# Attention pieces woven into an MLP: one piece per slot, and product drains issued ahead of the woven pieces

## The chip, the cores and the metric

The kernel runs on one core of a Trainium2 chip. The metric is device time in microseconds (us) of one execution. Most tables quote the median of all executions of a kernel.

For differences below 1% I rely on *batch lengths*: the time from the first up-projection matmul of a batch (tile `ph`) to that of the next, read from the timeline. Of the kernel before there is one, and at 594.98 us it was faster than every one of its timed executions (595.57 to 601.82 us).

## The reference, cut to what matters

```python
q_n, k_n = rmsnorm(q, g_q), rmsnorm(k, g_k)         # q, k, v: 8 batches, 12 heads, 448 tokens, 64 dims
attn = softmax(scale * q_n @ k_n.T)                 # per head
x = (attn @ v)  -> (8, 448, 768)
h = x.transpose(0, 2, 1) @ U @ V                    # low-rank mixing over tokens, rank 32
u = x + h.transpose(0, 2, 1)
out = u + np.maximum(u @ w_ch1, 0) @ w_ch2          # 768 -> 3072 -> 768
```

## The kernel before

TensorE (PE) is the scarce engine. The MLP of batch b is written as a Python generator that yields after every six matmuls; `weave` runs it and, between yields, issues pieces of the attention of batch b+1, in proportion to their weights. A *slot* is the place between two weighted pieces. `FA` is the share of the MLP's work over which attention is spread; the low-rank mixing of batch b+1 follows over a share of 0.09. Each engine has a queue of its own, filled in the order in which the code issues instructions; the timelines below show VectorE (DVE) working in that order.

The down-projection of an odd batch, and two of the three token tiles of an even one, uses seven products instead of eight per pair of token tiles, with sums of weights (`weight_sums`, once, in batch 1) and of activations (`act_sums`) on DVE. Each product has a *drain*, the instructions that take its PSUM tile away.

```python
def product(ps, lhs, rhs, first, last, again=False):
    for c in range(NC):                              # 12 matmuls
        nc.tensor.matmul(ps, lhs[:, c, :], rhs[:, c, :], ...)
        if c % 6 == 5:
            yield HALF                               # also after the last one: pieces come before the drain

def pair(b, i, then=None):
    ...
    yield from product(pa, A12, B21, False, True, True)
    nc.vector.tensor_tensor(A12, A12, A11, OP.subtract)
    o11 = out_tile(); nc.vector.tensor_add(o11, pa, X[0][0]); store(b, i, 0, o11)
    yield from product(pb, A21, B12, False, True, True)
    o22 = out_tile(); nc.vector.tensor_add(o22, pb, se)
    nc.gpsimd.tensor_tensor(o22, o22, X[1][1], OP.add); store(b, i + 1, 1, o22)
    if then:
        then()                                       # act_sums for the second pair of tiles
    yield from product(pe, A12, B22, False, True, True)
    ...

def attention(b, extra={}):                          # p: pair of heads, t = p // 2: their loaded tile
    for p in range(b * 6, b * 6 + 6):
        add(2 if p == 6 else 1, scores, p, (0, 1)); add(0, expo, p, 0); add(.5, expo, p, 1)
        add(.5, transposes, p + 1)                   # from p + 1 = 14 on: a transposing DMA on the sync queue
        ...                                              # cut here and below: mix_u, loads, casts
        if t + 1 < NT and not odd: add(0, reduce, t + 1, ALL, (1,))      # row sum of squares of K
        if p % 6: add(2, values, p - 1, 0)
        add(0, gains, p + 1)                         # qkT *= gg on DVE: waits for that DMA
        if t + 1 < NT and odd: add(0, scale, t + 1, 1) ...
        add(1, scores, p, (2, 3)); add(0, expo, p, 2); add(.5, expo, p, 3)
        if t + 1 < NT and not odd: add(0, rsqrt, t + 1)
        if p % 6: add(1.5, values, p - 1, 1)
        if t + 1 < NT and not odd:
            add(0, scale, t + 1, 0) ...; add(0, squares, t + 2, ALL, (0,))
        if p in (12, 13, 14):                        # four weight sums at a time, eight at p = 14
            for i in range(4): add(0, weight_sums, ...)
        if t + 2 < NT and odd:
            add(0, reduce, t + 2, ALL, (0,)); add(0, squares, t + 2, ALL, (1,))
```

## Time and profile before

| | before |
|---|---|
| time, median | 597.1 us |
| span of the profiled execution | 593.2 us |
| PE / DVE / ScalarE (ACT) busy | 96% / 66% / 47% |
| head (up to the first `ph`) | 45.84 us |
| batches 0 to 7 | 66.89, 79.27, 62.94, 74.74, 62.95, 74.74, 63.42, 62.39 us |

Even batches have 384 tokens to work on and odd ones 512, so the lengths alternate; batch 1 also carries the weight sums, and batch 7 has no attention to weave.

From the page of the kernel before: its span, the first line of part 1 (busy us, share, instructions) and of part 4 (the chain of work that ended last, by engine).

```profile
span 593.2 us, 11361 instructions
...
PE 568.0 (96%) x4613; PEld 312.9 (53%) x4613; DVE 393.1 (66%) x811; ACT 278.6 (47%) x413; POOL 85.9 (14%) x122
...
PE 74%; DVE 14%; ACT 4%; DMA 3%; issue 2%; POOL 1%; DVEq 0%; ACTq 0%; POOLq 0%; SPq 0%
```

PE looks full. It is not: a quarter of the chain runs elsewhere. The list of waits of PE says what it waited for (us in total, times, longest one); note that it leaves out the pieces of a wait that the modelled end of the matmul before covers, so the true holes are some 0.15 us longer each.

```profile
PE ph L468 <- DVE hT L473: 3.4, 5, 1.2
PE sc L273 <- ACT E L278: 2.4, 6, 0.6
PE ph L468 <- DMA u<-x: 1.8, 3, 1.1
PE o L299 <- DVE xs L306: 1.7, 1, 1.7
...
PE pb L404 <- DVE o L434: 1.3, 3, 0.4
```

The fourth line and the longest wait of the first, 1.2 us in batch 1, come from the weight sums; the rest of the first line is 0.5 to 0.8 us each in batch 0 and the even batches. The timeline of DVE in batch 1 (start, us, line, operation, count) shows a burst of four sums, then a row sum, and the ReLU `hT` that PE waits for only behind both. PE stood still for 1.3 us up to 134.9 us.

```profile
130.38 2.75 DVE L394 TENSOR_TENSOR Tw<-w2b,Tw 128x1152 bf16<-128x1152 bf16 x4
133.05 1.21 DVE L231 TENSOR_REDUCE rstd<-sq 112x16 f32<-112x1024 f32 x1
134.18 0.68 DVE L473 TENSOR_SCALAR hT<-ph 128x512 bf16<-128x512 f32 x1
```

The line for `pb` is one wait in each odd batch. Timeline of DVE, and below it the matmuls that wait: the product `pb` was done before 308.7 us (`pe`, the next one, starts at 308.65), but its drain (`o<-pb,se`) runs at 310.60, behind three instructions of a values piece and a row sum.

```profile
308.85 0.18 DVE L302 RECIPROCAL rec<-o 128x4 f32<-128x4 f32 x1 [0.59 <-PE o L299]
309.06 0.36 DVE L303 TENSOR_TENSOR x<-o,rec 128x192 bf16<-128x192 f32 x1
309.34 0.21 DVE L306 TENSOR_TENSOR xs<-o,rec 64x64 bf16<-64x64 f32 x1
309.47 1.20 DVE L231 TENSOR_REDUCE rstd<-sq 112x16 f32<-112x1024 f32 x1
310.60 0.54 DVE L434 TENSOR_TENSOR o<-pb,se 128x384 f32<-128x384 f32 x1
...
311.19 1.14 PE L404 MATMUL pb<-Tw,hT 128*128 128x384 bf16 x6 [0.43 <-DVE o L434]
```

### The profile page before, as it was taken

How to read it: one execution, taken by the hardware profiler on the slowest of the kernel's cores; microseconds unless marked ns; L12 is line 12 of the kernel's file. 1: busy time of each engine (PE TensorE's matmuls, PEld its weight loads, DVE VectorE, ACT ScalarE, POOL GpSimd, SP SyncE). 2: the span in 40 equal slices, each digit the busy share in tenths (PEclk: the TensorE clock that was granted, in tenths of full speed). 3: DMA queues.
4: the chain of work that ended last, by engine and by line, in shares of the span. 5: the costliest groups of instructions: out<-in, count | busy, mean ns of one | idle time of the engine just before them, and what ended most of it. 6: DMA issues, size and time to landing. Idle time of an engine off the chain costs nothing.

```text
span 593.2 us, 11361 instructions
## 1 busy us (share of the span) xinstructions
PE 568.0 (96%) x4613; PEld 312.9 (53%) x4613; DVE 393.1 (66%) x811; ACT 278.6 (47%) x413; POOL 85.9 (14%) x122
## 2 busy tenths in 40 slices
PE   6899999998899999999999999999999999999997
PEld 2465555544465555644456555644455555654464
DVE  6968886388875678737767487757667577453452
ACT  5846662257531676256541576336662366302200
POOL 5652420023020000000010000100002000000010
PEclk9999999999999999999999999999999999999999
DMA  9999989342454345644526345555335432040021
GB/s 212 236 240 236 216 152 189 92 109 32 109 142 100 82 95 133 147 99 109 125 77 127 85 113 123 136 122 125 80 61 157 100 94 33 28 108 0 1 51 56
DMA packets 103648, 67.22 MB, mean 113 GB/s; under 512 B 54716, under 2 KB 102060, under 8 KB 103596
## 3 DMA queue, kind: packets, MB, share of 16 engines
q1 hardware_dynamic: 93988, 56.77, 41.4%
q0 software_dynamic: 9376, 9.44, 9.7%
q8 instruction: 36, 0.59, 0.4%
q10 hardware_dynamic: 232, 0.30, 0.2%
q14 instruction: 16, 0.13, 0.1%
HBM read 52.19 MB, written 11.01 MB: 107 GB/s over the span
## 4 chain that ended last, share of the span: by engine, by line
PE 74%; DVE 14%; ACT 4%; DMA 3%; issue 2%; POOL 1%; DVEq 0%; ACTq 0%; POOLq 0%; SPq 0%
PE ph L468 27%; PE pb L404 10%; PE pa L404 7%; PE o L299 7%; PE po L404 7%; PE pe L404 6%; PE sc L273 5%; DVE rstd L231 3%; DVE qkn L244 3%; ACT E L278 2%; PE pu L337 2%; DMA u<-x 2%; DVE Tw L394 1%; DVE x L303 1%; DVE hT L473 1%
## 5 line engine op out<-in xcount | busy, mean ns | idle before, releaser
L468 PE MATMUL ph<-u,w1b 128*128 128x512 bf16 (+1 forms) x1128 | 232.9, 353 | 5.4 <-DVE hT L473 3.4
L278 ACT ACTIVATE E<-sc 112x896 bf16<-112x896 f32 x184 | 159.5, 915 | 45.1 <-PE sc L273 44.4
L468 PEld LDWEIGHTS <-w1b 128*128 128x128 bf16 x1128 | 103.2, 98 | 111.5 <-issue 25.6
L404 PEld LDWEIGHTS <-hT 128*128 128x128 bf16 x1080 | 101.2, 98 | 72.9 <-issue 9.7
L471 ACT ACTIVATE hT<-ph 128x384 bf16<-128x384 f32 (+1 forms) x95 | 51.5, 544 | 140.4 <-PE ph L468 135.8
L473 DVE TENSOR_SCALAR hT<-ph 128x512 bf16<-128x512 f32 (+1 forms) x93 | 57.9, 623 | 50.5 <-PE ph L468 49.9
L299 PEld LDWEIGHTS <-E 112*128 112x128 bf16 x1472 | 58.3, 98 | 17.4 <-DVE xs L306 3.5
L223 ACT ACTIVATE sq<-qk 112x1024 f32<-112x1024 f32 x36 | 37.8, 1049 | 58.2 <-DVE rstd L231 40.2
L273 PE MATMUL sc<-qkT 64*112 64x448 bf16 x384 | 60.8, 374 | 3.7 <-ACT E L278 2.4
L681 POOL COPY scratch<-qkn 1x1 bf16<-1x1 bf16 x44 | 18.3, 416 | 314.9 <-DVE qkn L244 313.4
L244 DVE TENSOR_TENSOR qkn<-qk,rstd 112x512 bf16<-112x512 f32 x84 | 56.3, 709 | 10.4 <-issue 6.0
L299 PE MATMUL o<-va,E 112*128 112x65 bf16 x1440 | 61.0, 194 | 1.7 <-DVE xs L306 1.7
L404 PE MATMUL po<-w2b,hT 128*128 128x384 bf16 x288 | 52.2, 326 | 0.6 <-DVE hT L473 0.6
L231 DVE TENSOR_REDUCE rstd<-sq 112x16 f32<-112x1024 f32 x40 | 48.5, 1212 | 4.9 <-ACT sq L223 3.7
L404 PE MATMUL pa<-w2b,hT 128*128 128x384 bf16 x264 | 49.5, 326 | 0.0
L404 PE MATMUL pb<-Tw,hT 128*128 128x384 bf16 x264 | 48.0, 326 | 1.3 <-DVE o L434 1.3
L302 DVE RECIPROCAL rec<-o 128x4 f32<-128x4 f32 x96 | 17.1, 178 | 35.6 <-PE o L299 35.4
L273 PEld LDWEIGHTS <-qkT 64*112 64x112 bf16 x384 | 19.6, 124 | 36.8 <-issue 31.9
L303 DVE TENSOR_TENSOR x<-o,rec 128x192 bf16<-128x192 f32 x96 | 34.3, 358 | 3.7
L435 POOL TENSOR_TENSOR o<-o,x 128x384 f32<-128x384 f32 x11 | 12.6, 1146 | 160.6 <-DVE o L434 160.6
L339 DVE TENSOR_TENSOR x<-pu,x 128x768 bf16<-128x768 f32 (+1 forms) x27 | 23.3, 866 | 8.2 <-PE pu L337 7.9
L404 PE MATMUL pe<-Tw,S 128*128 128x384 bf16 x132 | 24.3, 326 | 0.0
(106 smaller groups left out, 426.0 us busy)
## 6 DMA issues: line engine op xcount, KB each, us to landing
qk<-in_q_dram SPq DMA_DIRECT2D x21, 448.0 KB, 6.0
vt<-in_v_dram SPq DMA_DIRECT2D x20, 448.0 KB, 5.0
qk<-in_k_dram SPq DMA_DIRECT2D x19, 448.0 KB, 3.9
w2b<-in_moe_w_ch_dram POOLq DMA_DIRECT2D x6, 768.0 KB, 9.7
w1b<-in_moe_w_ch_dram POOLq DMA_DIRECT2D x2, 1536.0 KB, 22.3
out_dram<-o SPq DMA_DIRECT2D x15, 168.0 KB, 2.6
out_dram<-o SPq DMA_DIRECT2D x16, 144.0 KB, 2.1
out_dram<-o SPq DMA_DIRECT2D x15, 120.0 KB, 2.0
```

Source lines behind the costliest of these rows:

```text
L223: nc.scalar.activation(sqs[t, s][:, hs], qks[t, s][:, hs], AF.Square)
L231: nc.vector.tensor_reduce(rstds[t][:, s, hs].rearrange("p h j -> p (h j)"), sqs[t, s][:, hs].rearrange("p h (j d) -> p (h j) d", d=D), AX, ...
L244: nc.vector.tensor_tensor(qkn[:, s].rearrange("p j h d -> p h j d"), qks[t, s][:, hp].rearrange("p h (j d) -> p h j d", d=D), rstd[:, s, h ...
L273: nc.tensor.matmul(sc[:, hh, 0:S], kT[pp, kc * SP:(kc + 1) * SP], qT[pp, :], start=True, stop=True)
L278: nc.scalar.activation(E_of(p)[:, :, PAD + kc * S:PAD + (kc + 1) * S], scs.pop((p, kc))[:, :, 0:S], AF.Exp, scale=float(D) ** 0.5)
L299: nc.tensor.matmul(o[:, i, :], E[:, hh, c:c + P], va[:, hl, kc, :], start=(kc == 0), stop=(kc == NJ - 1))
L303: nc.vector.tensor_tensor(x3[:, :, d0:d0 + D], o[:, t0:t0 + 3, 0:D], rec[:, t0:t0 + 3].rearrange("p c -> p c ()").to_broadcast([P, 3, D]), ...
L339: nc.vector.tensor_add(xv, pu[rows, 0:n, 0:HALF], xv)
L404: nc.tensor.matmul(ps, lhs[:, c, :], rhs[:, c, :], start=first and c == 0, stop=last and c == NC - 1, skip_group_check=again)
L468: nc.tensor.matmul(ph, w1b[:, dc, hc * P:(hc + 1) * P], u[:, dc, :], start=(dc == 0), stop=(dc == KD - 1))
L471: nc.scalar.activation(hT[:, hc, 0:n], ph, AF.Relu)
L473: nc.vector.tensor_relu(hT[:, hc, 0:n], ph)
```

## The change

Its intent is to break up bunches. Seven things move (the share, the drains, the weight sums, squares, row sums, gains and transposes); no arithmetic is added or removed.

```diff
-    FA, FM, NPE, FA0 = 0.77, 0.09, 14, 0.66
+    FA, FM, NPE, FA0 = (0.74, 0.77), 0.09, 14, 0.66          # even, odd batches
 def product(...):
-            if c % 6 == 5:
+            if c == 5:                                         # the yield at the end moves to the callers,
                 yield HALF                                     # behind each drain:
 def pair(b, i, then=None):
         nc.gpsimd.tensor_tensor(o22, o22, X[1][1], OP.add)
         store(b, i + 1, 1, o22)
         if then:
             then()
+        yield HALF
         yield from product(pe, A12, B22, False, True, True)
  ...    (the same after every other drain, in pair, single and batch 0)
 def attention(b, extra={}):
+        def sums(p, n):                                        # one weight sum at each of four places
+            f = {12: 0, 13: 1, 14: 3, 15: 2}.get(p)
+            if f is not None:
+                add(0, weight_sums, f, 3 * n)
  ...
-            if p + 1 < NP:
+            if p + 1 < NP and (p + 1 >= NPE or not odd):
                 add(.5, transposes, p + 1)
-            if t + 1 < NT and not odd:
-                add(0, reduce, t + 1, ALL, (1,))
+            sums(p, 0)
+            if not odd and more:
+                add(0, squares, t + 1, ALL, (1,))              # squares of K, one slot later than before
+            if odd and more2:
+                add(0, squares, t + 2, ALL, (0,))
             if p % 6:
                 add(2, values, p - 1, 0)
-            if p + 1 < NP:
-                add(0, gains, p + 1)
+            sums(p, 1)
+            if not odd and more:
+                add(0, reduce, t + 1, ALL, (1,))
  ...        (scores, p, (2, 3) and their exponentials)
+            if p + 1 < NPE and odd:
+                add(.5, transposes, p + 1)
+            if p + 1 < NP:
+                add(0, gains, p + 1)                           # gains half a piece later
+            sums(p, 2)
             if p % 6:
                 add(1.5, values, p - 1, 1)
+            sums(p, 3)
  ...
-            if p in (12, 13, 14): (weight sums in bursts)
-            squares (t + 2, Q) and (t + 2, K) at the end of a pair of heads
```

More of the change, by code (lines that the diff above doesn't have):

```diff
@@ L424, in pair @@
         nc.scalar.activation(se, pe, AF.Copy)
+        yield HALF
         yield from product(pb, A11, T2, False, True, True)
         nc.vector.tensor_add(pe, pb, se)
+        yield HALF
         yield from product(pa, A12, B21, False, True, True)
@@ L431, in pair @@
         store(b, i, 0, o11)
+        yield HALF
         yield from product(pb, A21, B12, False, True, True)
@@ L438, in pair @@
             then()
+        yield HALF
         yield from product(pe, A12, B22, False, True, True)
@@ L442, in pair @@
         store(b, i, 1, o12)
+        yield HALF
         yield from product(pb, A22, T4, False, True, True)
@@ L446, in pair @@
         store(b, i + 1, 0, o21, (nc.sync, nc.scalar) if b == B - 1 else (nc.sync,))
+        yield HALF
     def single(b, i):
@@ L454, in single @@
             yield from product(po, A1, BQ(0, half), True, False)
+            yield HALF
             yield from product(po, A2, BQ(1, half), False, True)
@@ L460, in single @@
             store(b, i, half, o)
+            yield HALF
     def mlp(b):
@@ L482, in mlp @@
                         yield from product(po, hTe[:, :, k, i * P:(i + 1) * P], BQ(k, half), k == 0, k == 1)
+                        if k == 0:
+                            yield HALF
                     o = out_tile()
@@ L485, in mlp @@
                     store(b, i, half, o)
+                    yield HALF
         elif par:
@@ L498, in add @@
             items.append((weight, lambda: fn(*args)))
+        def sums(p, n):
+            f = {12: 0, 13: 1, 14: 3, 15: 2}.get(p)
+            if f is not None:
+                add(0, weight_sums, f, 3 * n)
         for p in range(b * 6, b * 6 + 6):
             t, odd = divmod(p, 2)
+            more, more2 = t + 1 < NT, t + 2 < NT
             add(2 if p == 6 else 1, scores, p, (0, 1))
@@ L508, in attention @@
                 add(0, mix_u, 0, p - 7, (0,))
-            if t + 1 < NT and not odd:
-                add(0, reduce, t + 1, ALL, (1,))
+            sums(p, 0)
[3 more added lines that the diff above has]
+                add(0, squares, t + 2, ALL, (0,))
             if p % 6:
                 add(2, values, p - 1, 0)
-            if p + 1 < NP:
-                add(0, gains, p + 1)
-            if t + 1 < NT and odd:
+            sums(p, 1)
+            if not odd and more:
+                add(0, reduce, t + 1, ALL, (1,))
+            if odd and more:
                 add(0, scale, t + 1, 1)
@@ L527, in attention @@
             add(.5, expo, p, 3)
-            if t + 1 < NT and not odd:
-                add(0, rsqrt, t + 1)
+            if p + 1 < NPE and odd:
+                add(.5, transposes, p + 1)
             if 7 <= p <= 10:
                 add(0, mix_u, 0, p - 7, (1,))
+            if p + 1 < NP:
+                add(0, gains, p + 1)
+            if not odd and more:
+                add(0, rsqrt, t + 1)
+            sums(p, 2)
             if p % 6:
                 add(1.5, values, p - 1, 1)
-            if t + 1 < NT and not odd:
+            sums(p, 3)
+            if not odd and more:
                 add(0, scale, t + 1, 0)
                 add(0, yield_port, t + 1, 0)
-                add(0, squares, t + 2, ALL, (0,)) if t + 2 < NT else None
-            if p in (12, 13, 14):
-                for i in range(4):
-                    add(0, weight_sums, (0, 1, 3)[p - 12], 3 * i)
-                    if p == 14:
-                        add(0, weight_sums, 2, 3 * i)
-            if t + 2 < NT and odd:
+            if odd and more2:
                 add(0, reduce, t + 2, ALL, (0,))
-                add(0, squares, t + 2, ALL, (1,))
             if p in extra:
@@ L731 @@
             if b + 1 < B:
-                rest = [(4, lambda: (load_w2(0, 0), transposes(6), reduce(4, ALL, (0,)), squares(4, ALL, (1,))))] + attention(1, late)
-                weave(fill, total * (FA if b else FA0), attention(b + 1) if b else rest)
+                rest = [(4, lambda: (load_w2(0, 0), transposes(6), reduce(4, ALL, (0,))))] + attention(1, late)
+                weave(fill, total * (FA[b % 2] if b else FA0), attention(b + 1) if b else rest)
                 weave(fill, total * FM, mixing(b + 1))
```

## The prediction

> **What bounds the kernel.** The page: PE busy 568.0 of 593.2 us (96%), DVE 66%, ACT 47%, clock full. The chain that ended last: 74% PE, 14% DVE, 4% ACT, 3% DMA. The Trainium skill ("Perfetto Trace Analysis", Identifying the Most-Contended Engine) calls matmul busy time a poor measure of headroom; the trace agrees: ends are modelled, and a 96% busy PE still waits. I took the gaps between matmul starts (timeline). In a filled stretch one starts every 216 ns (512 columns) or 162 ns (384). Against that pace there are short holes around scores (0.23 us per group of four, whatever the order) and real waits, after 66 us some 16 us:
> - Weight sums (bursts of four, 2.7 us on DVE) hold up ReLU drains behind them: PE waits 1.3 us at 134.9, 0.5 at 137, 1.8 at 150.8.
> - At 91-99 us ACT sits 5.3 us in front of squares whose K load is under way; the low-rank eviction behind it is late: 0.7 us on PE.
> - In every even batch two row sums and a square surround one drain: 0.65 and 0.75 us (209, 211.5; 346.6, 349), 1.0 us at 484.6; at its start Ln/Exp, squares and exponentials bunch on ACT: 0.5 us.
> - In every odd batch a drain of pb stands behind reciprocal, scaling and row sum: 0.59 us (173.5, 311.2, 448.9).
> - From even to odd batch PE waits for the transposing load of u: 0.5, 0.5, 1.3 us (255, 392.6, 530.8).
>
> The mechanism is queue order: the same page says (Tensor Engine Instruction) that ACT and DVE are strict FIFO; the trace agrees (the pb drain was ready, but ran after the 1.2 us row sum).
>
> **What the change does.** No arithmetic is added or removed: as many matmuls, row sums (1.21 us), squares (1.05), scalings (0.65), weight sums (0.67). Moved: product drains ahead of woven pieces; row sums, squares, scalings, weight sums into slots of their own (a ReLU drain now stands between two row sums); K squares a slot later, after their load; gains later, past their DMA transpose (DVE waited 8.4 us there); in even batches attention ends at 0.74 of the work instead of 0.77, some 1.3 us earlier (estimate: 3% of about 44 us of matmuls), so u is ready.
>
> **How much is critical.** Expected back: weight sums 3 of 3.7 us; squares 0.7; even-batch bunches 4.5 of 6.5; pb drains 1.6 of 1.8; u loads 2 of 2.3. About 12 us; less 2 us for attention packed 4% tighter in even batches and new bunches. Other DVE and ACT time is off the critical path. The head (60 us) stays.
>
> Prediction: 587 us (1.7% faster), 8 in 10 between 582.5 and 592.5. Faster by over 2% (below 585.2): 0.30; within 2%: 0.68; slower: 0.02.
>
> **What would show it.** Busy times unchanged to 1%. In the list of waits, ph for DVE hT falls from 3.4 us to under 1, ph for the load of u from 1.8 to under 0.5, pb for DVE o from 1.3 to near 0; the xs wait of 1.7 us is gone. An even plus an odd batch (193 to 330 us, 137.6) takes about 135 us. The stretch 103-155 us shrinks by about 3 us.
>
> **What would make it wrong.** Pairs of batches shorter by under 1 us: new bunches replaced the old, expected in even batches, on scores waiting for exponentials (2.4 us now). A gain above 15 us: the holes around scores depend on order after all. Drains put first could also block an engine that waits for PE there.

## The result and the profile after

| | before | after |
|---|---|---|
| time, median (range) | 597.13 (596.44 to 598.74) us | 587.35 (586.19 to 588.01) us |
| ratio after / before, 95% interval | | 0.983 (0.9804 to 0.9857) |
| span of the profiled execution | 593.2 us | 584.4 us |
| head | 45.84 us | 46.07 us |
| batches 0 to 3 | 66.89, 79.27, 62.94, 74.74 | 64.78, 75.33, 61.85, 74.86 |
| batches 4 to 7 | 62.95, 74.74, 63.42, 62.39 | 61.86, 74.87, 62.40, 62.39 |

Ratios are the mean time of one kernel's runs over that of the other's of the same rounds, so not quite the ratio of the medians quoted. The result is 1.7% faster, 9.8 us by the medians.

The page after, the same lines:

```profile
span 584.4 us, 11372 instructions
...
PE 565.6 (97%) x4613; PEld 313.4 (54%) x4613; DVE 395.0 (68%) x811; ACT 279.1 (48%) x413; POOL 78.3 (13%) x122
...
PE 82%; DVE 11%; ACT 4%; issue 1%; DMA 1%; POOL 1%; DVEq 0%; POOLq 0%; ACTq 0%
```

PE, DVE and ACT are as busy as before, within 1%, and the chain runs more through PE. The list of PE's waits after has none of `ph` for `hT`, none of `ph` for `u` and none of `pb`. But it has new lines, `sc` for `rec` and for `qkT`, and the wait for `xs` is as large as it was, in three parts:

```profile
PE sc L273 <- DVE rec L302: 2.1, 3, 0.9
PE sc L273 <- DVE qkT L265: 1.7, 3, 0.6
PE o L299 <- DVE xs L306: 1.6, 3, 0.5
PE sc L273 <- ACT E L278: 1.2, 4, 0.4
```

In batch 1 the weight sums now stand two by two between other work (timeline of DVE), and the ReLU comes through:

```profile
117.98 1.42 DVE L394 TENSOR_TENSOR Tw<-w2b 128x1152 bf16<-128x1152 bf16 x2
119.31 1.29 DVE L244 TENSOR_TENSOR qkn<-qk,rstd 112x512 bf16<-112x512 f32 x2
120.52 0.69 DVE L482 TENSOR_SCALAR hT<-ph 128x512 bf16<-128x512 f32 x1
```

In an odd batch the drain `o<-pb,se` is now early, at 301.71. Yet PE waits in the same stretch, one piece later: the activation sums (`S<-hT`, `hT<-hT`, 2.5 us together) stand in the code right behind that drain and came forward with it, ahead of the normalisation that the next values matmuls (`o<-va,E`) wait for.

```profile
301.71 0.54 DVE L438 TENSOR_TENSOR o<-pb,se 128x384 f32<-128x384 f32 x1
302.17 0.94 DVE L399 TENSOR_TENSOR S<-hT 128x1536 bf16<-128x1536 bf16 x1
303.15 1.55 DVE L400 TENSOR_TENSOR hT<-hT 128x1536 bf16<-128x1536 bf16 x1
304.63 0.17 DVE L302 RECIPROCAL rec<-o 128x4 f32<-128x4 f32 x1
304.83 0.36 DVE L303 TENSOR_TENSOR x<-o,rec 128x192 bf16<-128x192 f32 x1
305.10 0.20 DVE L306 TENSOR_TENSOR xs<-o,rec 64x64 bf16<-64x64 f32 x1
...
305.37 0.68 PE L299 MATMUL o<-va,E 112*128 112x65 bf16 x16 [0.54 <-DVE xs L306]
```

So odd batches gained nothing (74.74 to 74.87 us). In even batches a new wait of scores stands behind a row sum: `qkT` gets its gains (L265) only after the row sum, whose squares were issued in the slot just before it, and the score matmuls wait for `qkT`.

```profile
327.15 1.22 DVE L231 TENSOR_REDUCE rstd<-sq 112x16 f32<-112x1024 f32 x1 [0.93 <-ACT sq L223]
328.28 0.33 DVE L265 TENSOR_SCALAR qkT<-qkT,gg 128x448 bf16<-128x448 bf16 x1
...
328.76 0.80 PE L273 MATMUL sc<-qkT 64*112 64x448 bf16 x4 [0.56 <-DVE qkT L265]
```

A second wait of this kind comes some 9 us later in each even batch, with activation sums in front of the gains. The list puts it down to `rec`, but the scores start 0.15 us after the end of the gains, as above (0.15 us), and `rec` is only the next instruction behind the gains:

```profile
200.57 0.33 DVE L265 TENSOR_SCALAR qkT<-qkT,gg 128x448 bf16<-128x448 bf16 x1
200.82 0.17 DVE L302 RECIPROCAL rec<-o 128x4 f32<-128x4 f32 x1
...
201.05 0.58 PE L273 MATMUL sc<-qkT 64*112 64x448 bf16 x4 [0.60 <-DVE rec L302]
```

Where the 9.0 us between the first `ph` and the end went (547.33 to 538.34 us): batch 1 gave 3.94, batch 0 2.11, the three even batches 1.09, 1.09 and 1.02, the odd batches 3 and 5 cost 0.25 together, and batch 7 is unchanged. (Batch 0 would be 2.65 and batch 6 0.68 by r_after.) The total came out as predicted; the shares did not. The experiments ask which of the moves did what.

### The profile page after: what moved, and what is told of

It reads as the page before. It is cut to its first block, busy times and chain, and to the rows that moved or that the text cites. A ratio compares the mean times of both kernels' runs of the same rounds, so it can differ in the third digit from the quotient of the medians.

```text
span 584.4 us, 11372 instructions
## 1 busy us (share of the span) xinstructions
PE 565.6 (97%) x4613; PEld 313.4 (54%) x4613; DVE 395.0 (68%) x811; ACT 279.1 (48%) x413; POOL 78.3 (13%) x122
## 4 chain that ended last, share of the span: by engine, by line
PE 82%; DVE 11%; ACT 4%; issue 1%; DMA 1%; POOL 1%; DVEq 0%; POOLq 0%; ACTq 0%
PE ph L477 33%; PE pb L404 8%; PE po L404 8%; PE o L299 8%; PE pa L404 7%; PE sc L273 7%; PE pe L404 6%; ACT E L278 3%; DVE qkn L244 2%; PE pu L337 2%; DVE rstd L231 1%; PE warm L741 1%; DVE hT L400 1%; DVE S L399 1%; DVE x L303 1%
## 5 line engine op out<-in xcount | busy, mean ns | idle before, releaser
L702 POOL COPY scratch<-qkn 1x1 bf16<-1x1 bf16 x44 | 11.1, 251 | 312.0 <-DVE qkn L244 310.3
L302 DVE RECIPROCAL rec<-o 128x4 f32<-128x4 f32 x96 | 17.1, 178 | 29.2 <-PE o L299 29.0
L419 ACT ACTIVATE pb<-pa 128x384 f32<-128x384 f32 x11 | 5.2, 474 | 50.2 <-PE pa L404 50.2
```

## The experiments

Twelve kernels ran, all with correct results. In each group of four, kernels and the kernel before ran on the same chip.

| run | what | median us | ratio to before (95%) | batches 0 to 6, us |
|---|---|---|---|---|
| e1_sums | before + weight sums spread | 593.74 | 0.9944 (0.9912 to 0.9976) | 66.91 75.72 62.94 74.73 63.00 74.74 64.11 |
| e2_drains | before + early drains | 602.13 | 1.008 (1.005 to 1.011) | 67.41 79.28 65.87 74.59 64.96 74.59 63.41 |
| e3_fa | before + share 0.74 | 595.89 | 0.9972 (0.9947 to 0.9997) | 67.08 79.11 63.10 74.74 63.25 74.74 62.31 |
| e4_slots | before + pieces reordered | 590.70 | 0.9902 (0.9866 to 0.9939) | 64.79 77.26 62.56 74.73 62.55 74.73 63.78 |
| e10_store_late | e2_drains, stores late | 601.28 | 1.0086 (1.0053 to 1.0119) | 69.23 79.60 64.18 74.58 63.52 74.58 64.12 |
| e8_undo_drains | after without early drains | 586.89 | 0.9817 (0.9788 to 0.9847) | 64.59 75.20 62.00 74.75 62.00 74.74 62.31 |
| e9_fa77 | after with share 0.77 | 593.03 | 0.9926 (0.9894 to 0.9957) | 64.23 75.33 63.76 74.87 62.78 74.88 63.98 |
| e5_then | after, activation sums later | 586.73 | 0.9828 (0.9795 to 0.9861) | 64.52 74.62 61.86 74.15 61.86 74.15 62.99 |
| r_after | after again | 589.31 | 0.9852 (0.981 to 0.9894) | 64.24 75.34 61.87 74.87 61.87 74.87 62.74 |
| e12_drains_share | e2_drains + share 0.74 | 596.19 | 0.9978 (0.9942 to 1.0015) | 67.57 79.44 62.87 74.58 63.01 74.58 62.44 |
| e13_then_gains | e5_then, gains early | 595.87 | 0.9967 (0.9926 to 1.0008) | 64.54 74.55 67.03 74.15 68.23 74.15 63.52 |
| e14_odd_drains | e5_then, early drains in odd batches only | 586.98 | 0.9815 (0.9778 to 0.9852) | 64.60 74.61 62.52 74.15 62.35 74.15 62.29 |

### e1_sums: the weight sums alone

```diff
+            sums(p, 0) ... sums(p, 3)        # one per slot, p = 12 to 15
-            if p in (12, 13, 14): four (eight) weight_sums in a row
```

> Before, with the weight sums alone spread (four head pairs, one sum of 0.67 us per slot). Theory S (bursts of DVE sums were the largest single loss): batch 1 (79.3 us from its first up-projection matmul to that of batch 2 in before, 75.3 in after) falls by 3.0 to 3.9 us, other batches by under 0.2; total about -3.5 us. Rival I (the sums only hurt together with row sums and squares that share their slot): under -1.5 us alone.

Batch 1 fell by 3.55 us and no other batch but batch 6 moved by more than 0.1; the median fell by 3.5. Theory S holds: the bursts cost this by themselves. (Batch 6 is 0.7 us longer through a longer wait for the load of `u`, which varies between executions of one kernel: 62.40 and 62.74 us in two of the kernel after.)

### e2_drains: the early drains alone

```diff
-            if c % 6 == 5:
+            if c == 5:
                 yield HALF
+        yield HALF                           # behind each drain, in pair, single and batch 0
```

> Before, with the drains of products issued ahead of the woven pieces and nothing else. Theory D (prediction): PE no longer waits 0.59 us for the pb drain in each odd batch, total -1.5 to -2 us. Rival W (read from the trace of after): the activation sums for the second pair of tiles (2.5 us of DVE) now also stand ahead of the woven normalisation, a wait of 0.7 us of values for xs takes its place, and odd batches stay at 74.7 us; total within 0.5 us of before.

Neither expectation held for the total: the kernel became 4.9 us slower. For odd batches the rival W was right (74.74 to 74.59 us: the wait for the drain is gone, a wait for `xs` is there). What nobody expected is batch 2, 2.9 us longer, and batch 4, 2.0 us longer. The gaps between matmul starts place the loss of batch 2: values wait 1.5 us for `xs`, `pb` 0.6 us, and the first `ph` of batch 3 waits 1.1 us longer for `u` than before.

The first of these led to the sync queue (SP), which issues both the output stores and the transposing load of `qkT`. Its timeline, for the kernel before, whose batch 2 starts at 192.0 us:

```profile
232.97 1.22 SPq L261 DMA_TRANSPOSE qkT<-qkn  x1
234.40 0.89 SPq L380 DMA_DIRECT2D out_dram<-o  x2
```

and for e2_drains, whose batch 2 starts at 192.7 us, with the matmuls that came late:

```profile
235.12 0.81 SPq L380 DMA_DIRECT2D out_dram<-o  x2
236.03 1.22 SPq L261 DMA_TRANSPOSE qkT<-qkn  x1
...
241.88 0.69 PE L299 MATMUL o<-va,E 112*128 112x65 bf16 x16 [1.32 <-DVE xs L306]
```

The list of waits of that queue in e2_drains, from 230 to 243 us, has in front:

```profile
SPq L380 <- DVE o L467: 9.7, 1, 9.7
```

With the drain the store moved ahead, the queue sat 9.7 us in front of that store until its tile was made, and the transposing load behind it was issued 2.3 us later in the batch. The gains on DVE then waited 2.6 us for it, and everything behind them.

### e3_fa: the share alone

```diff
-    FA = 0.77
+    FA = (0.74, 0.77)
```

> Before, with attention of even batches spread over 0.74 of the work instead of 0.77. Theory F: the waits for the load of u at the start of odd batches (0.5, 0.5, 1.3 us) go, -2.0 us in all, even batches 62.95 to about 62.45 us, the seventh (b6) 63.4 to 62.2. Rival: the 4% denser attention gives it back in even batches by ACT and DVE bunches, total within 0.5 us.

Mixed. The waits for `u` are gone, and batch 6 fell by 1.1 us. But batches 2 and 4 became 0.16 and 0.30 us longer: what the load gave back, denser attention took (scores waiting for exponentials, and a ReLU on ACT). From -2 us expected, -1.4 came by the medians.

### e4_slots: the reordered pieces alone

```diff
-  squares(t + 2, Q), squares(t + 2, K) at the end of a pair; reduce, then values, then gains
+  squares(t + 2, Q) and squares(t + 1, K) in slots of their own; values, then reduce; gains behind scores (2, 3)
+  transposes of odd pairs after scores (2, 3)
```

> Before, with the attention pieces reordered (row sums, squares, scalings, gains, transposes), weight sums left in bursts, drains and shares as before. Theory: batch 0 falls by 2.1 us (K squares after their load, transposes of odd pairs later), even batches by about 0.6 us each (two row sums apart, but score matmuls now wait 0.7 us twice for the gains on DVE), odd batches under 0.2; total -4 us. Rival (reordering is the main part): -6 us or more, with even batches at 61.9 without the new share. If the parts add up, the four runs sum to about -9.5 us.

This is the largest single part, -6.6 us by the medians and -4.5 by the traces from the first `ph` to the end (the one profile of the kernel before was a fast execution): batch 0 by 2.1, batch 1 by 2.0 (the row sums no longer stand behind a burst of weight sums, so half of that loss goes even with the bursts left in), and batches 2 and 4 by 0.4 each (batch 6, with a longer wait for `u`, not at all). The even batches get so little because of the new waits of scores: 0.94 us in two parts at the start and 0.76 us some 9 us on, which are there in this run as in the kernel after. By the medians the four parts sum to -6.7 us against the -9.8 of the whole change, by the traces to -2.8 against -9.0: they are not independent, and the early drains are the odd one out.

### e10_store_late: is it the store on the sync queue?

```diff
         o11 = out_tile(); nc.vector.tensor_add(o11, pa, X[0][0])
-        store(b, i, 0, o11)
         yield HALF
+        store(b, i, 0, o11)                  # and so after every other drain
```

> The early drains alone (e2_drains, 602.1 us) with one thing taken back: the output stores are issued after the woven pieces again, as in before, only the arithmetic of the drains stays ahead. Theory Q (the store ahead of the transposing load of qkT holds up the sync queue, in order, until its drain is done; the gains, the scores and the values behind it come late): the +2.9 and +2.0 us of batches 2 and 4 go, total 596 to 598 us. Rival V (the vector and scalar work of the drains itself, ahead of the pieces, costs it): stays above 600 us.

Theory Q held for the batches that it was about and failed as the explanation of the total. Batches 2 and 4 are 1.7 and 1.4 us shorter than in e2_drains. The effect: the sync queue again waited for `qkn`, as it did in the kernel before, not for the drain; the load of `qkT` is back at its old place in the batch (41.0 us after its start, as before, against 43.3 in e2_drains); and in the second half of batch 2 no wait for `xs` is left. From the lists of waits of the queue and of PE:

```profile
SPq L261 <- DVE qkn L244: 8.2, 1, 8.2
...
PE ph L477 <- DMA u<-x: 1.7, 1, 1.7
```

But the wait of the second line stayed and grew (the hole is 1.8 us against 1.6 in e2_drains, and 1.2 against 0.6 in front of batch 5), batch 0 became 2.3 us longer than before (1.8 longer than in e2_drains), and the kernel was no faster than e2_drains. Why batch 0 is longer I did not settle; batch 0 also differs by 0.5 us between two executions of one kernel. The loads of `u` led to the next theory: early drains also stand ahead of the additions of the low-rank mixing on DVE, which make the tiles that those loads read. Times of the last two issues of `u`, before the last matmul of batch 2: 4.53 and 2.11 us in the kernel before, 3.35 and 2.05 in e2_drains, 3.82 and 1.42 in e10_store_late.

### e8_undo_drains and e9_fa77: the change without one part

```diff
 e8_undo_drains:   product(), pair(), single() and batch 0 of the kernel before
 e9_fa77:
-    FA = (0.74, 0.77)
+    FA = (0.77, 0.77)
```

> After, with the drains behind the woven pieces again as in before; slots, weight sums and shares as in after. If the parts added up (-3.5, -6.6 and -1.4 us alone, from 597.3), 585.5 us, faster than after by 2 us. Rival X (the parts interact: with the gains late and the share at 0.74 the early drains do no harm and help): 587 to 589 us.

> After, with attention of even batches over 0.77 of the work again. If the share is worth in after what it was alone: +1.4 to 2 us, waits for the load of u back at 0.5, 0.5 and 1.3 to 1.5 us. Rival: with the drains early and 0.77 the late stores and transposes of e2_drains come back, +4 us or more, even batches at 64 us or above.

Without the early drains the kernel is as fast as with them: from the first `ph` to the end 537.99 us against 538.34, and the ratio's interval covers that of the kernel after. So the early drains as they stand in the change are worth nothing in the end, neither for nor against (e5_then below shows what they are worth without the line that came along). Neither expectation for e8_undo_drains is refuted by the times alone (586.89 us lies between 585.5 and the 587 of X), but the batches say why: even ones 0.14 longer, odd ones 0.12 shorter, which cancel.

The share of 0.74 is worth about 4 us in the changed kernel (batches 2, 4 and 6 are 1.91, 0.92 and 1.58 us longer without it) although it was worth 1.4 alone. The waits for `u` are 1.55, 0.61 and 1.73 us in these batches, against none, none and 0.24 in the kernel after. That is more than the first expectation; the rival's loss of 4 us or more is there, though its even batches of 64 us were not quite reached.

### e12_drains_share: early drains and the share together

```diff
 e2_drains, and
-    FA = 0.77
+    FA = (0.74, 0.77)
```

> Before with two parts together: early drains (alone 602.1 us) and attention of even batches over 0.74 (alone 595.9). Theory M (early drains delay the additions of the low-rank mixing on DVE and so the transposing loads of u: the last two of an even batch are issued 3.35 and 2.05 us before its last matmul instead of 4.53 and 2.11; the share of 0.74 starts the mixing 1 us earlier and pays for that): the loss of the drains goes, 594 to 597 us, even batches 62.9 to 63.3 us. Rival (plain sum of the parts): 600.7 us, even batches 65 us.

The loss of the early drains is gone, as theory M expected: even batches are 62.87, 63.01 and 62.44 us. The last two issues of `u` are at 5.45 and 3.03 us before the last matmul of the batch instead of 3.35 and 2.05, and there is no wait for it in batches 2 and 4. A plain sum of the parts would have been 600.7. But that theory M is the whole cause is not shown, since the share took away the other loss too: the load of `qkT` is issued 41.1 us after the start of batch 2, as in e10_store_late (41.0) and not as in e2_drains (43.3), and the wait of 1.5 us for `xs` behind it is gone. The sync queue waits for `qkn` again and not for a store (230 to 246 us):

```profile
SPq L261 <- DVE qkn L244: 8.7, 1, 8.7
```

By the holes in e2_drains the queue made the larger part of the loss: in batch 2 2.1 us (`xs` and `pb`) against 1.1 for the load of `u`, in batch 4 2.1 against 0.1. What is shown is that the share of 0.74 pays for the early drains. And the drains add nothing to it: 1.4 us by the medians for the two together here, 1.4 for the share alone in e3_fa.

### e5_then: the line that came along

```diff
         store(b, i + 1, 1, o22)
+        yield HALF
         if then:
             then()
-        yield HALF
```

> After, with one line moved: the activation sums for the second pair of tiles (2.5 us of DVE) are issued after the woven piece, not ahead of it with the drains. Theory W: the 0.7 us wait of values for xs in batches 1, 3 and 5 goes, odd batches 74.87 to 74.2 us, total -2 us (585.3). Rival: another piece takes the wait over and odd batches stay within 0.2 us.

Theory W holds to the number in the trace: odd batches are 74.15 us, 0.72 shorter than in the kernel after, batch 1 0.7 shorter, and the wait for `xs` is gone. Against e8_undo_drains, which differs from it by the early drains alone, batches 1, 3 and 5 are 0.58, 0.59 and 0.59 us shorter: without the sums in front, the early drains are worth 1.8 us, close to the 1.6 of the prediction. By the medians the gain does not show, since the load of `u` of batch 6 took longer (a wait of about 0.8 us) in the profiled execution and some executions ran with a slowed head: 586.73 us, against 587.35 in the first and 589.31 us in the third group for the kernel after. Of the executions whose mean clock was at least 0.999, three of e5_then took 584.81, 584.85 and 585.78 us, two of r_after 586.32 and 586.52.

### r_after, e13_then_gains and e14_odd_drains

> The changed kernel once more, unedited, as the yardstick for the other three of this call: 586 to 588 us, batches 61.85 and 74.87 us as before, apart from the length of the head and the wait for the load of u in b6, which vary from execution to execution.

As expected but for batch 0, 0.54 us shorter than in the first profile, and for the median, which is higher because four of its six executions had a mean clock of 0.986 to 0.997.

```diff
 e13_then_gains (on e5_then):
             if p % 6:
                 add(2, values, p - 1, 0)
+            if p + 1 < NP:
+                add(0, gains, p + 1)
  ...
-            if p + 1 < NP:
-                add(0, gains, p + 1)        # behind scores (2, 3)
```

> e5_then with the gains on qkT back ahead of the second pair of score groups, as in before. Theory G (moving the gains late put them behind a row sum or the activation sums on DVE, and scores wait 0.93 and 0.77 us in every even batch): batches 2, 4 and 6 fall from 61.86 to about 60.3 us, total -4 us against e5_then. Rival (early gains block DVE until the DMA transpose lands, as in before, where DVE waited 8.4 us): even batches 62 us or longer, total the same or worse.

Theory G failed and its rival won, by far: batches 2 and 4 became 5.2 and 6.4 us longer. DVE's wait for the transposing loads, 8.4 us in the kernel before and 2.3 in the kernel after, rose to:

```profile
DVE qkT L265 <- DMA qkT<-qkn: 36.1, 23, 5.5
```

The loads land 2.9 to 7.4 us after issue (median 3.2), and the gains, waiting for them in order, hold up the row sum, the ReLU and the normalisation behind. The late place costs at most 1.7 us in an even batch (the waits of scores above) and saves far more. It is not a pure undo: in the kernel before the row sum stood ahead of the gains, here behind them. In batch 2, after PE had waited 2.5 us, its clock was halved for 3.4 us, and 1.7 of the 5.2 us are the slower matmuls there (229.70 to 233.90 us, 4.2 us for work that takes 2.5 at the full pace). A wait as long at 371.5 us, in batch 4, was not followed by that. From the view of stretches, this run from 228 to 236 us (PEclk is the number before the last two):

```profile
228.00:236.00 8.00, 6.79 (x46) 3.51 (x47) 6.55 (x15) 3.69 (x6) 0.78 (x1) 0.79 0.17 33
```

```diff
 e14_odd_drains (on e5_then):
-  yields behind the drains everywhere
+  yields behind the drains in odd batches; in batch 0 and even ones at the end of each product, as in before
```

> e5_then with the early drains kept in odd batches only; in batch 0 and the even ones they stand behind the woven pieces as in before. Theory M: the last transposing load of u is issued 4.6 us before the last matmul of an even batch instead of 3.0, batch 6 no longer waits for u (62.3 us where after and e5_then had 62.4 and 63.0), the other even batches 62.0, odd batches 74.15 as in e5_then; 1.5 to 2.5 us faster than r_after. Rival (early drains are worth something in even batches too): even batches longer by 0.3 us or more.

Half right. The loads of `u` are issued 4.57 us before the last matmul and batch 6 no longer waits (62.29 us), but batches 2 and 4 are 62.52 and 62.35, half a microsecond longer than in e5_then; so the rival's mark of 0.3 us is passed. But they are also longer than the 62.00 of e8_undo_drains, whose even batches are written alike, so the missing early drains are not the main reason. In batch 2 the trace shows one: a load of `qkT`, issued 14.74 us after the start of the batch in both, landed 7.3 us after issue, in e8_undo_drains 6.4. The gains waited 1.93 us for it instead of 1.00, and the scores behind them left a hole of 0.62 us that e8_undo_drains does not have. In the fourteen profiled executions the loads in this place of batch 2 took 5.6 to 7.3 us. From e14_odd_drains and, below, e8_undo_drains:

```profile
211.20 0.34 DVE L265 TENSOR_SCALAR qkT<-qkT,gg 128x448 bf16<-128x448 bf16 x1 [1.93 <-DMA qkT<-qkn]
211.68 0.58 PE L273 MATMUL sc<-qkT 64*112 64x448 bf16 x4 [0.45 <-DVE qkT L265]
```

```profile
209.60 0.34 DVE L265 TENSOR_SCALAR qkT<-qkT,gg 128x448 bf16<-128x448 bf16 x1 [1.00 <-DMA qkT<-qkn]
```

In batch 4 it was a pause of 0.46 us on DVE between `rec` and the normalisation, with no cause that the trace shows; the wait of the scores some 5 us later is 0.35 us longer. From the first `ph` to the end it is 537.07 us, against 536.54 of e5_then and 538.17 of r_after. Both beat the kernel after in the trace by about 1 to 1.6 us; the intervals of the times overlap, so on time they are the same.

## Why the prediction was right or wrong, point by point

The total was right, 587 against 587.35 us, and in part by luck: the terms erred both ways. Even-batch bunches and pb drains gave some 5 us less than counted, batches 0 and 1 over 2 us more, and the 2 us taken off for new bunches covered most of the rest.

- **Weight sums, 3 of 3.7 us: right.** e1_sums alone gave 3.55. In the whole change batch 1 gave 3.94; the parts overlap, since e4_slots alone took 2.0 us off the same batch.
- **Squares behind the K load, 0.7 us: mis-sized.** Batch 0 gave 2.1 us, in e4_slots and in the whole. The prediction took only the one wait at 99.7 us; in the reordered kernels the shorter holes around the transposes at 70.9, 71.5, 87.0 and 87.6 us of the kernel before (1.3 us together) are gone as well. (So are 0.40 us at 56.5 and 0.62 at 67.6, for three new holes of 0.9 us together.)
- **Even-batch bunches, 4.5 of 6.5 us: wrong.** The step that failed is the overlap of the moved gains with the scores. Reordering alone gave 0.4 us in each of batches 2 and 4. The two old waits around the drain are gone, but scores now wait 0.94 and 0.77 us for the gains on DVE. The prediction had counted "gains later" as free slack. It did name a new bunch in even batches as the main danger, but on scores waiting for exponentials; that wait fell (2.4 to 1.2 us), and it was the gains.
- **pb drains, 1.6 of 1.8 us: wrong.** Zero, or slightly negative. The drain is early, and the wait of 0.6 us became one of 0.7 us on values, because the activation sums moved with the drain. e5_then shows it by taking them out, and with them out the early drains give 1.8 us (against e8_undo_drains). The prediction's diff reading stopped at the drain and did not ask what else stands between it and the new yield.
- **Loads of u, 2 of 2.3 us: right in size, and incomplete in cause.** After, 0.24 us is left of 2.3. But alone the share gave back part of it (e3_fa), and the early drains by themselves make those loads later (the second-last 3.35 instead of 4.53 us before the last matmul in e2_drains), which the prediction missed.
- **Order as the mechanism: right.** It cited the Trainium skill ("Perfetto Trace Analysis", Tensor Engine Instruction) for ACT and DVE being strict FIFO. The timelines agree: 301.71 to 305.30 us in the kernel after is one queue in order. What bit hardest was a third such queue, the sync engine's, on which a store waited 9.7 us and held up a load.
- **What would show it.** Busy times: PE, DVE, ACT within 1%, POOL not (85.9 to 78.3 us, a rough span on an idle engine). `ph` for `hT`, `ph` for `u` and `pb` for `o` fell as said. The `xs` wait did not: 1.7 us in one piece became 1.6 in three, in other places. The stretch named there, 103 to 155 us, became 3.9 us shorter (between the same two matmuls of the MLP), where about 3 were forecast. An even plus an odd batch took 136.7 us, not 135: the windows below, before (batches 2 and 3) and after, cut to 0.1 us (columns: stretch, us, busy PE, PEld, DVE, ACT, POOL, clock, DMA share, GB/s).

```profile
192.00:254.94 62.94, 61.35 (x535) 35.43 (x532) 45.60 (x95) 34.16 (x51) 5.50 (x10) 1.00 0.54 118
254.94:329.68 74.74, 74.26 (x568) 38.85 (x568) 48.81 (x100) 36.43 (x53) 7.07 (x11) 1.00 0.47 106
```

```profile
186.24:248.10 61.86, 60.69 (x534) 35.52 (x533) 45.68 (x94) 34.10 (x51) 4.90 (x10) 1.00 0.54 121
248.10:322.96 74.86, 74.27 (x570) 38.76 (x569) 49.61 (x100) 36.51 (x53) 7.06 (x11) 1.00 0.48 104
```

- **What would make it wrong.** "Pairs of batches shorter by under 1 us: new bunches replaced the old" came true (0.96 us), and so did "drains put first could also block an engine that waits for PE there", on the sync queue. The total held because batches 0 and 1 gave 6 us where 3.7 had been counted for them.

## What to carry to other kernels

When instructions are moved forward, list everything that moves with them and every in-order queue they sit on: here a drain brought 2.5 us of activation sums ahead on DVE, and a store ahead of a load on the sync queue. Add the parts of a change one by one, and take them away one by one, since a part that loses 5 us alone (early drains) may be neutral inside the whole, paid for by another part (the share). A piece that waits for a DMA should stand late in an in-order queue: here the late place of the gains cost at most 1.7 us per even batch, the early one 5.2 and 6.4 us more than the late one in two of three (1.7 of the 5.2 at a halved clock).

## What the Trainium skill lacked or had wrong

- "Perfetto Trace Analysis", Per-instruction lifecycle, DMA Instruction — HWDGE, has the sequencer wait for its semaphores before it issues, and calls it free for the next instruction only at the end. It does not spell out the consequence seen here: a store that waits on the sync queue holds up an independent load behind it, 9.7 us of waiting and a load issued 2.3 us later (e2_drains).
- "TensorE: Matmul & The Clock Gate", Part 1, gives 215.7 ns between matmul starts of 512 columns; the traces agree (216 ns). It ties a slow clock to the first few microseconds and to idle windows of about 3.4 us, and calls the penalty of that ramp under 1% of a typical span. In e13_then_gains a wait of PE of 2.5 us was followed by a halved clock for 3.4 us, and another of the same length was not. And the clock was halved for 17.1 us from 21 us on in one execution of e1_sums, for 3.4 to 6.8 us near 20 to 29 us in e8_undo_drains, e13_then_gains and e14_odd_drains, and not in the heads of the other profiled executions. The head of e1_sums took 51.9 us, against 45.8 in the kernel before. That is 1% of the span, as large as the effects studied. What sets it off there, no run here tells. (Long slow stretches as such are not missing: the caveats there tell of a clock stuck low for over 50 us.)
- "DMA: Bandwidth & Descriptors", DMA Transpose (X-bar), gives constraints but no time to landing for a small transpose, and I found none on another page. Here those of `qkT` (112 by 1024 elements, 2 bytes each) landed 2.9 to 7.9 us after issue over all profiled executions, median 3.2.
